# Identity matmuls in a layer's tail and head, an earlier gather, and one wq row ahead of the first scores

## The chip, the cores and the metric

The kernel runs on one core of a Trainium2 chip. The metric is the device time of the program in microseconds (us), taken over several runs. One core has no second core to compare with, so a run counts as fast when it lies within 1.5% of the fastest of its kernel. Executions of one kernel in one call lie up to 4.2 us apart (busy16_only below: 1984.76 to 1988.94).

## The reference, cut to what matters

Four attention blocks for one token: caches A, B, A, B. Each normalises x, makes q from wq, attends to 32 heads of 8192 keys of 192 numbers, and projects by wo.

```python
x = x + _A_ref(_layernorm(x), A_k_cache, A_v_cache, A_wq, A_wo)   # layer 0
x = x + _B_ref(_layernorm(x), B_k_cache, B_v_cache, B_wq, B_wo)   # layer 1
x = x + _A_ref(_layernorm(x), ...)                                # layer 2
x = x + _B_ref(_layernorm(x), ...)                                # layer 3
```

With one token nothing of K and V is used twice within a layer: the program reads 848 MB from HBM.

## The kernel before

Heads go in 16 pairs. For each pair, VectorE (DVE) multiplies K by q in place; TensorE (PE) adds up the products by matmuls with the identity; softmax; PE multiplies by V; DVE picks and PE gathers ("e"); wo is applied in pieces. Loads go through one queue in a fixed order, each as soon as its slot is free. The order of steps at a layer's start and end is a list (cuts marked, comments added):

```python
elif l == 2:
    plan += [("wq", l, g) for g in range(3)]
    steps.append(("wq", l, 0))            # two wq rows ahead of the first scores
...
steps.append(("m", l, p, 0))              # DVE products and PE sums, first half of the keys
if l == 2 and p == 0:
    steps.append(("wq", l, 1))
...
steps.append(("m", l, p, 1))
if l == 2 and p == 0:
    steps.append(("wq", l, 2))
...
plan.insert(-2, ("wo", l, 2))
steps.append(("e", l, p - 1))             # gather of pair 14
steps += [("v", l, p, 0), ("wc", l, 2)] if NB[l] else [("wc", l, 2), ("v", l, p, 0)]
steps += [("wo", l, 2), ("v", l, p, 1)]
if NB[l]:                                 # layers 1 and 3
    plan.append(("vq", l))                # last quarter of pair 15's V
    both(("wob", l))                      # second part of the last large wo piece
steps.append(("e", l, p))                 # gather of pair 15
both(("wol", l))                          # last wo piece, into the row that "wc" frees
```

In layer 2 the slots of the K halves and of the wq pieces are what the next loads go into: the first V load waits for the sums of the first half of K, the third wq piece for the first wq piece's rows.

```python
PE.wait(last["S"][u], ev_const)
for c in range(4):
    PE.wait(chunks[c])                    # a piece of DVE's products
    ...                                   # 6 identity matmuls a piece, 24 in all
freed[nt] = ev_S[p, u] = e                # frees the K half
```

Of the kernel before, what the change touches and what calls it, by code (L numbers as in the profile page):

```python
# [68 lines left out]
def build(nc, A_x, A_k, A_v, A_wq, A_wo, B_x, B_k, B_v, B_wq, B_wo, out):  # L69
    _, H, SK, DH = A_k.shape  # L70
    D = A_x.shape[-1]
    P = 128
# [17 lines left out]
    NB = [0, 5, 0, 5]  # L90
# [7 lines left out]
    with ExitStack() as ctx:  # L98
# [9 lines left out]
        ident = sb("ident", [P, P], BF16)  # L108
# [40 lines left out]
        SP_ = [ps("S0"), ps("S1")]  # L149
# [6 lines left out]
        Su = [(use["S0"],), (use["S1"],)]  # L156
# [60 lines left out]
        def both(*ns):  # L217
            plan.extend(ns)
            steps.extend(ns)

        for l in range(NL):
            if l < 2:
                plan.append(("wq", l, 0))
                steps += [("wq", l, g) for g in range(3)]
            elif l == 2:
                plan += [("wq", l, g) for g in range(3)]
                steps.append(("wq", l, 0))
            else:
                both(("wq", l, 0))
            for p in range(NPAIR):  # L230
                if first_load("k", l, p) == (l, p):
                    plan += [("k", l, p, u) for u in range(2)]
                if stays("k", l, p):
                    plan += [("t", l, p, u) for u in range(2)]
                steps.append(("m", l, p, 0))
                if l == 2 and p == 0:
                    steps.append(("wq", l, 1))
                if l == 2 and p == 1:
                    steps.append(("e", l, 0))
                steps.append(("m", l, p, 1))  # L240
                if l == 2 and p == 0:
                    steps.append(("wq", l, 2))
                if p == NPAIR - 1:
                    steps.append(("v", l, p - 1))
                steps.append(("s", l, p))
                if l == 3 and p == 0:
                    both(("wq", l, 1), ("wq", l, 2))
                if p < NPAIR - 2:
                    if first_load("v", l, p) == (l, p):
                        plan += [("v", l, p, u) for u in range(2)]  # L250
                        if l == 2 and p == 1:
                            i = plan.index(("k", l, 1, 0))
                            plan[i - 1:i + 1] = [("k", l, 1, 0), ("v", l, 0, 1)]
                    steps.append(("v", l, p))
                    if l != 2 or p > 0:
                        steps.append(("e", l, p))
                    if p + 1 in (PAIRS_W, 2 * PAIRS_W):
                        b = (p + 1) // PAIRS_W - 1
                        steps.append(("wc", l, b))
                        both(("wo", l, b))  # L260
            for i in (p - 1, p):
                if first_load("v", l, i) == (l, i):
                    plan += [("v", l, i, u) for u in range(2)]
            plan.insert(-2, ("wo", l, 2))
            steps.append(("e", l, p - 1))
            steps += [("v", l, p, 0), ("wc", l, 2)] if NB[l] else [("wc", l, 2), ("v", l, p, 0)]
            steps += [("wo", l, 2), ("v", l, p, 1)]
            if NB[l]:
                plan.append(("vq", l))
                both(("wob", l))  # L270
            steps.append(("e", l, p))
            both(("wol", l))
        at = {n: i for i, n in enumerate(steps)}

# [137 lines left out]
        ev_true = DV.op(lambda v: v.tensor_copy(x_true[:], x_bf[:]), ev_x)  # L412
        ev_z = DV.op(lambda v: v.tensor_copy(z[:], x_bf[:]), ev_x)

        def sums(ev_z):

            DV.wait(ev_z, last["st"])
            DV.op(lambda v: v.tensor_reduce(st[:, 0:1], z[:], AX.X, ALU.add))
            e = DV.op(lambda v: v.scalar_tensor_tensor(out=zz[:], in0=z[:], scalar=1.0, in1=z[:],
                                                       op0=ALU.mult, op1=ALU.mult, accum_out=st[:, 1:2]))  # L420
            e = PE.op(lambda t: t.matmul(TB[:, C_ST:C_ST + 2], lhsT=ones[:, 0:1].broadcast_to([P, P]), rhs=st[:], start=True, stop=True),
                      e, ev_const, last["stt"], bank=TBu)
            last["st"] = e
            e = DV.op(lambda v: v.tensor_scalar(mv[:], TB[:, C_ST:C_ST + 2], 1.0 / D, None, ALU.mult), e, last["rs"], bank=TBu)
            last["stt"] = e
            return e

        def layer(l, ev_z, ev_true):

            ev_mv = sums(ev_z)  # L430
            if l == 0:
                ev_z = DV.op(lambda v: v.tensor_scalar(z[:], z[:], mv[:, 0:1], None, ALU.subtract), ev_mv)
                ev_mv = sums(ev_z)
            ev_xb = DV.op(lambda v: v.tensor_scalar(xb[:], z[:], mv[:, 0:1], None, ALU.subtract),
                          ev_mv, ev_z, last["xb"])
            e = DV.op(lambda v: v.scalar_tensor_tensor(out=nv[:], in0=mv[:, 0:1], scalar=mv[:, 0:1], in1=mv[:, 1:2],
                                                       op0=ALU.mult, op1=ALU.subtract))
            e = DV.op(lambda v: v.tensor_scalar(vs[:], nv[:], -float(DH), float(DH) * EPS, ALU.mult, ALU.add), e, last["rs"])
# [16 lines left out]
            for c in range(DC):  # L455
                for h in range(2):
                    e = PE.op(lambda t, c=c, h=h: t.matmul(
                        QM[64 * h:64 * h + 64, 0:DH], lhsT=xb[:, c:c + 1].broadcast_to([P, 64]),
                        rhs=q_first[:, c, h * DH:(h + 1) * DH], start=(c == 0), stop=(c == DC - 1)),
                        signal=(c == DC - 1 and h == 1), bank=QMu)  # L460
            ev_q = {}
            i0 = l * NPAIR % 2
            ev_q[0] = last["QB"] = AC.op(
                lambda a: a.activation(q_sb[i0][:], QM[:, 0:DH], ACT.Copy, scale=rs[:, 0:1]),
                e, ev_rs, last["q"][i0], bank=QMu)

            def q_rows(g):

                n = ("wq", l, g)
                c0, k = Q_PARTS[g]  # L470
                t3 = wq_rows(l, g)[:, :, ORDER[l]["q1"] * PD if l < 2 else 0:]
                PE.wait(need(("wq", l, 0)) if l < 2 else need(n), ev_xb, last["O"], last["YB"], ev_first.get(l))
                for c in range(k):
                    for b in range(4):
                        w = min(512, QR - b * 512)
                        for r in range(3):
                            fin = c0 + c == DC - 1
                            o, x, y = (OY[32 * r:32 * r + 1, b * 512:b * 512 + w], xb[:, c0 + c:c0 + c + 1],
                                       t3[:, c, r * QR + b * 512:r * QR + b * 512 + w])
                            e = PE.op(lambda t, b=b, c=c, r=r, o=o, x=x, y=y, fin=fin: (  # L480
                                t.matmul(o, lhsT=x, rhs=y, start=c0 + c == 0, stop=fin) if b == 0 else
                                matmul_held(t, o, x, y, c0 + c == 0, fin, 32, 32 * r)),
                                signal=(c == k - 1 and b == 3 and r == 2), bank=OYu)
                freed[n] = e
                if c0 + k == DC:
                    last["xb"] = e
                    last["rows"] = AC.op(
                        lambda a: a.activation(rows[0:65, :], OY[0:65, 0:QR], ACT.Copy, scale=rs[0:65, 0:1]),
                        e, ev_rs, last["qbc"], bank=OYu)
# [176 lines left out]
            for n in [n for n in steps if n[1] == l]:  # L666
                if n[0] == "m":
                    products(*n[2:])
                elif n[0] == "s":
                    softmax(n[2])  # L670
                elif n[0] == "v":
                    values(n[2], n[3:] or (0, 1))
                elif n[0] == "e":
                    gather(n[2])
                elif n[0] == "wq":
                    q_rows(n[2])
                    q_ready = n[2] == 2 or q_ready
                elif n[0] == "wc":
                    columns(NW)
                    last["oTw"] = last["TT"]  # L680
                elif n[0] == "wo":
                    k = NW - NB[l] if n[2] == 2 else NW
                    last["oT"] = project(n, slot[place[n]][:, 0:k * D], oT[:, 0:k], last["oTw"])
                elif n[0] == "wob":
                    last["oT"] = freed[("wo", l, 2)] = project(
                        n, slot[place[("wo", l, 2)]][:, (NW - NB[l]) * D:NW * D], oT[:, NW - NB[l]:NW], last["oTw"])
                else:
                    last["TT"] = last["TTn"]
                    last["oTl"] = ev_y = project(n, rows[:], oTl, last["TTn"])
                if q_ready and (n[0] == "wq" and l >= 2 or n[0] == "m" and n[3] == 1):  # L690
                    following = n[2] + 1 if n[0] == "m" else 1
                    if following < NPAIR and following not in ev_q:
                        q_spread(following)
                ahead()
# [64 lines left out]
```

## Time and profile before

| | kernel before |
|---|---|
| median of the first 3 runs | 1984.95 us |
| read from HBM | 848 MB at 428 GB/s |
| busy share of PE, DVE | 64%, 61% |
| seam of layers 1 and 2: second wo piece landed, third wq piece landed, first V load issued and landed | 1012.14, 1030.59, 1029.60, 1039.25 us |
| end: last V quarter landed, last DVE instruction ended | 1975.77, 1981.19 us |

A load runs on 16 DMA engines: in this trace 16 packets of the load queue were in flight for 1827.7 of 1982.3 us, and the 183 loads have 2928 semaphore updates, 16 each. "Landed" means the last of the 16. That each update stands for one engine is my reading; no record names an engine. The **hole** is (V load landed) - (third wq piece landed) - 7.30 us, where 7.30 is the spacing of two loads of that size in steady flow: the time that was lost on the slowest DMA engine between the two loads. The prediction works it out for the kernel before, 1.36 us. The **tail** is (last DVE instruction ended) - (layer 3's last V quarter landed), before 81.19 - 75.77 = 5.42 us.

This is the timeline of the kernel before (columns: start, us, engine, line, operation, out<-in, shapes, count, and in brackets the idle time before it and what ended it):

```profile
996.95 3.14 DVE L639 SCALAR_TENSOR_TENSOR acc<-OY,small,acc 128x192 f32<-128x192 f32 x7
...
1000.14 0.81 PE L650 MATMUL TB<-acc,small 128*1 128x192 f32 x4 [4.15 <-DVE acc L639]
...
1002.89 2.73 PE L620 MATMUL OY<-pool,p_sb 128*4 128x384 bf16 x32 [0.66 <-DMA pool<-in_B_v_cache_dram]
```

PE is idle for 4.15 us while DVE picks. At 1001.02 the clock falls to half, and the 32 value matmuls take 2.73 us.

### The profile page before, as it was taken

The page shows a single profiled execution, that of the slowest core. Times are in us where ns is not written, and L with a number is a line of the kernel's source. Part 1 is how long each engine was busy: PE and PEld are TensorE (multiplying, and loading weights), DVE is VectorE, ACT ScalarE, POOL GpSimd, SP SyncE. Part 2 cuts the span into 40 slices and gives each one's busy share as a digit, 9 for nine tenths or more (in the row PEclk, how much of TensorE's full clock was granted, in tenths as well). Part 3 has the DMA queues.
Part 4 walks back from the last instruction along what each step waited for, and adds up shares of the span by engine and source line. Part 5 has one row for each costly group of instructions (what it writes and reads, how often), then busy time and mean ns, then how long its engine had stood idle before and what let it go on. Part 6 is the DMA issues. An engine that isn't in the chain of part 4 may idle for free.

```text
span 1984.0 us, 13908 instructions
## 1 busy us (share of the span) xinstructions
PE 1273.4 (64%) x8310; PEld 150.1 (8%) x3266; DVE 1200.7 (61%) x1371; ACT 139.5 (7%) x461; POOL 4.5 (0%) x22
## 2 busy tenths in 40 slices
PE   3567567566466666665775665675676766656657
PEld 0001001000200100100020010010002001001001
DVE  3566467467166656556745565665664775665665
ACT  0000000000000000000010000000000000000000
POOL 0000000000000000000000000000000000000000
PEclk9787777777587787777876777878886887777777
DMA  9999999999999999999999999999999999999998
GB/s 412 438 430 431 431 437 429 431 430 431 433 435 431 432 429 436 430 431 432 427 388 433 430 430 430 432 430 430 431 431 427 435 432 434 430 432 432 432 431 353
DMA packets 26926, 849.25 MB, mean 428 GB/s; under 512 B 3184, under 2 KB 3184, under 8 KB 3952
## 3 DMA queue, kind: packets, MB, share of 16 engines
q1 hardware_dynamic: 26720, 848.38, 99.5%
q8 instruction: 45, 0.74, 0.2%
q14 instruction: 17, 0.14, 0.0%
q10 hardware_dynamic: 144, 0.00, 0.0%
HBM read 848.36 MB, written 0.00 MB: 428 GB/s over the span
## 4 chain that ended last, share of the span: by engine, by line
DMA 68%; DVE 15%; PE 15%; ACT 1%; issue 0%; SPq 0%
DMA pool<-in_B_k_cache_dram 27%; DMA pool<-in_A_v_cache_dram 20%; DMA pool<-in_A_k_cache_dram 14%; DVE pool L543 13%; PE S L58 6%; PE OY L58 5%; DMA pool<-in_B_v_cache_dram 4%; PE OY L620 3%; DMA pool<-in_B_wo_dram 2%; ACT p_sb L580 1%; DVE acc L639 1%; DMA pool<-in_A_wq_dram 1%; DVE s_sb L565 1%; PE OY L513 0%; PE S L556 0%
## 5 line engine op out<-in xcount | busy, mean ns | idle before, releaser
L543 DVE TENSOR_TENSOR pool<-pool,q_sb 128x3072 bf16<-128x3072 bf16 x512 | 861.2, 1753 | 241.5 <-DMA pool<-in_B_k_cache_dram 144.0
L58 PE MATMUL S<-pool,ident 128*128 128x512 bf16 x2944 | 789.1, 425 | 20.3 <-DVE pool L543 19.0
L650 PE MATMUL TB<-acc,small 128*1 128x192 f32 x240 | 82.1, 493 | 219.1 <-DVE acc L639 219.1
L556 PE MATMUL S<-pool,ident 128*128 128x512 bf16 x128 | 62.9, 491 | 213.6 <-DVE pool L543 213.6
L58 PE MATMUL OY<-pool,p_sb 128*16 128x512 bf16 x1920 | 197.0, 485 | 0.0
L638 DVE TENSOR_SCALAR acc<-OY,small 128x192 f32<-128x192 f32 x64 | 26.7, 418 | 274.2 <-PE OY L58 246.2
L620 PE MATMUL OY<-pool,p_sb 128*16 128x512 bf16 (+1 forms) x1216 | 147.5, 497 | 62.7 <-DMA pool<-in_A_v_cache_dram 56.4
L639 DVE SCALAR_TENSOR_TENSOR acc<-OY,small,acc 128x192 f32<-128x192 f32 x424 | 177.1, 418 | 14.9
L565 DVE TENSOR_REDUCE s_sb<-S 128x64 f32<-128x512 f32 x128 | 88.1, 688 | 69.4 <-PE S L58 69.4
L502 ACT ACTIVATE q_sb<-QM 128x192 bf16<-128x192 f32 x60 | 19.9, 331 | 954.8 <-PE QM L496 954.8
L661 ACT ACTIVATE rows<-TB,small 1x192 bf16<-1x192 f32 x120 | 43.2, 406 | 585.1 <-PE TB L650 585.1
L634 DVE RECIPROCAL small<-TB 1x2 f32<-1x2 f32 x64 | 11.2, 175 | 96.7 <-PE TB L595 75.2
L580 ACT ACTIVATE p_sb<-s_sb,small 64x128 bf16<-64x128 f32 x128 | 55.7, 435 | 161.9 <-DVE small L574 161.1
L556 PEld LDWEIGHTS S<-pool,ident 128*128 128x128 bf16 x128 | 13.0, 101 | 686.2 <-DVE pool L543 636.4
L595 PE MATMUL TB<-small,ones 128*1 128x2 f32 x120 | 11.4, 165 | 74.1 <-ACT p_sb L580 74.1
L620 PEld LDWEIGHTS OY<-pool,p_sb 128*16 128x16 bf16 (+1 forms) x1216 | 39.3, 107 | 203.6 <-issue 133.5
L570 PE MATMUL QM<-ident,m_bf 128*64 128x64 bf16 x128 | 14.1, 217 | 54.4 <-DVE m_bf L567 53.8
L650 PEld LDWEIGHTS TB<-acc,small 128*1 128x1 f32 x240 | 19.7, 101 | 311.4 <-DVE acc L639 283.9
L513 PE MATMUL OY<-oT,pool 128*128 128x1 bf16 x900 | 38.2, 178 | 3.5 <-ACT oT L528 2.8
L513 PEld LDWEIGHTS OY<-oT,pool 128*128 128x128 bf16 x900 | 37.1, 131 | 7.0 <-ACT oT L528 3.6
L574 DVE TENSOR_REDUCE small<-QM 128x1 f32<-128x64 f32 x64 | 14.4, 225 | 36.1 <-PE QM L570 36.1
L496 PEld LDWEIGHTS QM<-rows,one_b 1*64 1x64 bf16 x120 | 6.2, 100 | 350.7 <-issue 344.8
(59 smaller groups left out, 186.1 us busy)
## 6 DMA issues: line engine op xcount, KB each, us to landing
pool<-in_B_k_cache_dram SPq DMA_DIRECT2D x28, 6144.0 KB, 38.1
pool<-in_B_v_cache_dram SPq DMA_DIRECT2D x28, 6144.0 KB, 34.2
pool<-in_A_v_cache_dram SPq DMA_DIRECT2D x27, 6144.0 KB, 27.6
pool<-in_A_k_cache_dram SPq DMA_DIRECT2D x34, 3072.0 KB, 20.4
pool<-in_A_k_cache_dram SPq DMA_DIRECT2D x14, 6144.0 KB, 36.8
pool<-in_A_v_cache_dram SPq DMA_DIRECT2D x10, 3072.0 KB, 14.3
pool<-in_B_k_cache_dram SPq DMA_DIRECT2D x8, 3072.0 KB, 22.7
pool<-in_A_wo_dram SPq DMA_DIRECT2D x6, 2400.0 KB, 21.4
```

Of the source, the lines that this page charges most:

```text
L58: return t.add_instruction(mybir.InstMatmult(name=t.bass.get_next_instruction_name(), engine=mybir.EngineType.PE, ins=[t.lower_ap(rhs), t. ...
L502: lambda a: a.activation(q_sb[i][:], QM[:, 0:DH], ACT.Copy), e, last["q"][i], bank=QMu)
L513: e = PE.op(lambda t, i=i, c=c, f=y_first[0], fin=n[0] == "wol" and i == k - 1: t.matmul(YB[:, c:c + 1], lhsT=t3[:, i, c:D:DC], rhs=o[:, i ...
L543: e = DV.op(lambda v, d0=d0: v.tensor_tensor(k3[:, :, d0:d0 + QD], kin[:, :, d0:d0 + QD], q_sb[qi][:, d0:d0 + QD].unsqueeze(1).broadcast_t ...
L556: t.matmul(S[:, :], lhsT=ident[:], rhs=k3[:, :, d0:d0 + R], start=True, stop=fin) if d0 == 0 else
L565: lambda v, u=u: v.tensor_reduce(s[:, u * JU:(u + 1) * JU], SP_[u][:].rearrange("p (j r) -> p j r", r=R), AX.X, ALU.add), ev_S[p, u], last ...
L580: ev_p[p] = AC.op(lambda a, h=h, r=r: a.activation(p_sb[par][r, :, h], s[r, :], ACT.Exp, bias=negm[par][r, 0:1], accum_out=l_col[par][r, h ...
L620: t.matmul(o, lhsT=x, rhs=y, start=f, stop=fin) if c == 0 else
L638: v.tensor_scalar(acc[:], O[:, 0:DH], pick[:, 0:1], None, ALU.mult) if i == 0 else
L639: v.scalar_tensor_tensor(out=acc[:], in0=O[:, i * DH:(i + 1) * DH], scalar=pick[:, i:i + 1], in1=acc[:], op0=ALU.mult, op1=ALU.add)), e if ...
L650: e = PE.op(lambda t, h=h: t.matmul(TB[96:97, C_O + h * DH:C_O + (h + 1) * DH], lhsT=half[:, h:h + 1], rhs=acc[:], start=True, stop=True), ...
L661: last["TO"] = last["row_written"] = AC.op(lambda a, h=h: a.activation(orow[:, o0 + h * DH:o0 + (h + 1) * DH], TB[96:97, C_O + h * DH:C_O ...
```

## The change

Its intent: keep the TensorE clock up through the tails of layers 1 and 3 and raise it early in layer 2, and get the first scores of layer 2 done sooner, because a V load waits for them. The core of the diff (cuts marked, comments added):

```diff
                 if l == 2 and p == 0:
-                    steps.append(("wq", l, 1))
+                    steps += [("wqr", l, 0), ("wq", l, 1)]
...
-            steps.append(("e", l, p - 1))
+            steps += [("busy", l, 16), ("e", l, p - 1)] if NB[l] else [("e", l, p - 1)]
...
             if NB[l]:
                 plan.append(("vq", l))
+                steps.append(("e", l, p))
                 both(("wob", l))
-            steps.append(("e", l, p))
+            else:
+                steps.append(("e", l, p))
             both(("wol", l))
...
+        def busy(n):                      # n matmuls identity x identity into a score bank, result unused
+            PE.wait(ev_const, last["S"][0])
+            ...
@@ layer 2's normalisation
+            if l == 2:
+                busy(2)                   # after the sums
...
+            if l == 2:
+                busy(6)                   # after the first q
...
-            def q_rows(g):
+            def q_rows(g, r0=0, r1=None): # only rows r0 to r1 of a wq piece
...
-                freed[n] = e
+                freed.setdefault(n, e)    # row one frees its part of the slot
...
                     last["oTl"] = ev_y = project(n, rows[:], oTl, last["TTn"])
+                    if l == 1:
+                        busy(2)           # after the last projection of layer 1
```

More of the change, by code (lines that the diff above doesn't have):

```diff
@@ L413, in build @@
         ev_z = DV.op(lambda v: v.tensor_copy(z[:], x_bf[:]), ev_x)
+        def busy(n):
+            PE.wait(ev_const, last["S"][0])
+            for i in range(n):
+                PE.op(lambda t, i=i: (
+                    t.matmul(SP_[0][:, :], lhsT=ident[:], rhs=ident[:].unsqueeze(1).broadcast_to([P, 4, P]), start=True, stop=True)
+                    if i == 0 else
+                    matmul_held(t, SP_[0][:, :], ident[:], ident[:].unsqueeze(1).broadcast_to([P, 4, P]), True, True)),
+                    signal=False, bank=Su[0])
         def sums(ev_z):
@@ L472, in q_rows @@
                 PE.wait(need(("wq", l, 0)) if l < 2 else need(n), ev_xb, last["O"], last["YB"], ev_first.get(l))
-                for c in range(k):
+                r1 = k if r1 is None else r1
+                for c in range(r0, r1):
                     for b in range(4):
@@ L482, in q_rows @@
                                 matmul_held(t, o, x, y, c0 + c == 0, fin, 32, 32 * r)),
-                                signal=(c == k - 1 and b == 3 and r == 2), bank=OYu)
-                freed[n] = e
+                                signal=(c == r1 - 1 and b == 3 and r == 2), bank=OYu)
+                freed.setdefault(n, e)
                 if c0 + k == DC:
@@ L674, in layer @@
                     gather(n[2])
+                elif n[0] == "busy":
+                    busy(n[2])
+                elif n[0] == "wqr":
+                    q_rows(n[2], 1)
                 elif n[0] == "wq":
-                    q_rows(n[2])
+                    q_rows(n[2], 0, 1 if l == 2 and n[2] == 0 else None)
                     q_ready = n[2] == 2 or q_ready
```

## The prediction

> **What bounds the kernel now.** I read the page first, then the chain of waits in order of time, then the DMA share in small windows, then the timeline of the few places where that share falls.
>
> ```profile
> PE 1273.4 (64%) x8310; PEld 150.1 (8%) x3266; DVE 1200.7 (61%) x1371; ACT 139.5 (7%) x461; POOL 4.5 (0%) x22
> ...
> DMA  9999999999999999999999999999999999999998
> ...
> HBM read 848.36 MB, written 0.00 MB: 428 GB/s over the span
> ...
> DMA 68%; DVE 15%; PE 15%; ACT 1%; issue 0%; SPq 0%
> ```
>
> No compute engine is above 64%, while the DMA row is 9 in 39 of 40 slices and DMA is 68% of the chain. The 848 MB take the span. A change that moves no byte can gain only where the queues run dry. Looking in half-microsecond windows, I find three places: the launch, the seam between layer 1 and layer 2 (1005 to 1031 us), and the end (from 1972 us). The seams before layer 1 and before layer 3 show no hole.
>
> The windows around the middle seam and the end (columns: busy of PE, weight loads, DVE, ACT, POOL, then granted clock, DMA share, GB/s):
>
> ```profile
> 1005.00:1012.00 7.00, 6.45 (x105) 3.85 (x97) 0.39 (x2) 0.19 (x1) 0.00 (x0) 0.50 0.88 343
> 1012.00:1020.00 8.00, 4.49 (x64) 3.88 (x64) 3.28 (x13) 0.69 (x2) 0.55 (x1) 0.50 1.00 421
> ...
> 1024.00:1028.50 4.50, 4.50 (x20) 0.00 (x0) 4.50 (x3) 0.00 (x0) 0.00 (x0) 0.90 0.94 361
> 1028.50:1031.00 2.50, 2.50 (x29) 0.18 (x6) 2.50 (x3) 0.00 (x0) 0.00 (x0) 1.00 0.61 169
> ```
>
> The DMA share is 0.88, 0.94 and 0.61, and the granted TensorE clock is 0.50 through the whole tail of layer 1. Idle share times length: 0.12 x 7 + 0.06 x 4.5 + 0.39 x 2.5 = 2.1 us averaged over the 16 DMA engines. The timeline at the deepest hole:
>
> ```profile
> 1018.57 13.44 DVE L543 TENSOR_TENSOR pool<-pool,q_sb 128x3072 bf16<-128x3072 bf16 x8 [1.11 <-ACT q_sb L464]
> 1020.28 0.09 PEld L481 LDWEIGHTS OY<-pool,xb 128*1 128x1 bf16 x3 [2.56 <-DMA pool<-in_A_wq_dram]
> ...
> 1023.58 0.61 PE L556 MATMUL S<-pool,ident 128*128 128x512 bf16 x1
> 1023.68 0.34 SPq L376 DMA_DIRECT2D pool<-in_A_wq_dram  x1
> 1023.98 5.59 PE L58 MATMUL S<-pool,ident 128*128 128x512 bf16 x23
> ...
> 1029.60 0.34 SPq L371 DMA_DIRECT2D pool<-in_A_v_cache_dram  x1
> ```
>
> DVE multiplies K by q in eight pieces of 1.68 us from 1018.57, so the first half (four pieces) is ready at 1025.3. PE cannot start adding it up until 1023.58, because two wq rows at the half clock stand before it (12 matmuls of 512 columns each, 3.3 us together). It finishes at 1029.5; only then is the slot free and the next V load issued, at 1029.60, when the queues are already drying up. That load is on the path.
>
> **Which engine matters.** A transfer's landing is 16 semaphore updates, and the trace has their times. For the last wo piece of layer 1 they run from 1005.70 to 1012.14: the slowest DMA engine is 6.45 us behind the fastest. Of the 2.1 us above, most is idle time of engines that were ahead anyway. The slowest had its last wq piece landed at 1030.59, and the V load behind it landed at 1039.25. A full-speed load of that size takes 7.30 us (a steady spacing of landings in layer 2: 1045.99 to 1053.29), so its hole is 1039.25 - 7.30 - 1030.59 = **1.36 us**. That is the largest gain I see at the seam if the same engine stays the slowest.
>
> [...]
> - [...] granted clock is 0.5 or 1.0, in pieces of 3.41 us or multiples (1001.02 to 1024.91 is 23.89, seven windows at half).
> [...]
> - [...] The trace shows 45 packets of 16384 bytes of about 1.07 us, and smaller ones of 8192; the spread of landings jumps by about 1 us at the latter (at 425.6, 620.7, 800.0 and 981.2 us). So I take the lag to belong to particular engines in both halves, an inference.
>
> **The change, part by part.**
>
> 1. *Sixteen identity matmuls before the picking of pair 14*, in layers 1 and 3. DVE picks pair 14 from 996.49 to about 1000.1 (one instruction of 0.42 us, then seven in 3.14), and PE is free from 996.0 until 1000.14. At full clock a 512-column matmul takes about 0.22 us (23 in 5.13 us from 1031.45), so 16 take 3.5 us: they fit. They hold the clock up in the window that ended at 1001.02, so it falls one window later, near 1004.4. Then the first half of pair 15's values (32 matmuls from 1002.89, 2.73 us at half clock) may run in half the time. What follows waits for DMA anyway: the last quarter of V lands at 1010.20 and in layer 3 at 1975.77. The second half starts there, cold again, because in this trace no stretch of projection matmuls (75 of them filling 0.99 of a window at 1499) ever raised the clock. So on the path: 0. The wol and wq loads come about 1.3 us sooner, but only for engines that are ahead: 0.
>
> 2. *Gather of pair 15 before the second wo piece*. Before, at the end:
>
> ```profile
> 1977.59 0.42 DVE L638 TENSOR_SCALAR acc<-OY,small 128x192 f32<-128x192 f32 x1 [4.66 <-PE OY L620]
> 1977.74 1.08 PEld L513 LDWEIGHTS OY<-oT,pool 128*128 128x128 bf16 x25 [0.92 <-DMA pool<-in_B_wo_dram]
> ...
> 1978.83 0.96 PEld L646 LDWEIGHTS TB<-small,acc 128*64 128x64 f32 x12
> ...
> 1980.23 0.68 PEld L513 LDWEIGHTS OY<-oTl,rows 128*128 128x128 bf16 x15 [0.44 <-ACT oTl L656]
> ```
>
> The 25 projections (1.08 us) lie beside the DVE's two picks (to 1978.46) and delay the 12 gather matmuls by only 0.37. After: gather 1978.51 to 1979.55, ACT's 0.27 hidden, 25 + 15 projections at 43 ns = 1.72 plus the last one's latency 0.08, to 1981.38; before they ended at 1980.99. **+0.4 us** at the end, on the path. At the seam the same sum gives 1013.75 + 1.8 = 1015.6 against 1015.43: +0.15, and the second wq load, which waits for that wo slot, moves from 1013.3 to about 1014.9; engines ahead are done with the first wq at 1016.96, so it arrives in time.
>
> 3. *busy(2), busy(2), busy(6) around layer 2's normalisation*. At half clock a matmul is 0.43 us, so each pair is 0.86. After wol PE was free for 0.52 us, and between the sums and q for 0.52: if cold, each pair delays the chain by about 0.34. Then q starts at 1018.0 instead of 1017.06 (0.15 + 0.34 + 0.34), DVE at 1019.5. Six more (2.6 us cold) end about 1021.5; the first wq lands at 1020.24, so 1.2 us late. In return the window 1018.1 to 1021.5 is now full and the clock should rise near 1021.5 instead of 1024.91.
>
> 4. *Only one wq row before the first scores*. One row warm is 0.9 to 1.0 us: scores start at 1022.5 to 1023. PE then catches up with DVE (24 x 0.22 = 5.2), so the first half ends 1.47 us after the fourth DVE piece: 1019.5 + 6.75 + 1.5 = **1027.8**, against 1029.5. The V load issues there; from issue to first bytes was 1.3 us (1029.60 to 1030.9), so data come at 1029.1, before the slowest engine dries at 1030.59. Its hole closes nearly whole: **-1.2 us** (1.36 less a margin). The third wq part overwrites only row one's half of the slot, so it may issue at 1022.5 instead of 1023.68; hidden. The other rows move behind the scores (three rows, 2.8 us, 1027.8 to 1030.6, against 1031.2 before), so the second half is not delayed.
>
> Sum: -1.2 (seam) + 0.4 (end) = -0.8; 1984.95 - 0.8 = 1984.1 us.
>
> **Rivals.**
> - *All DMA engines' holes count, not only the slowest's*: if the lag moves among engines, closing the 2.1 us at the seam gains all of it. For: the idle share; against: the jumps sit at regular fetches. With a warm tail too: about 1982.5.
> - *A new wait at the seam*: the extra matmuls stay cold and hold back q, so DVE becomes the bound (its 6.75 us start later) and the V load still issues after 1029. For: seven windows at half clock; against: one wq row (1.7 us cold) is taken out before it. Gain 0.3, loss 0.4 at the end: about 1985.
> - *The clock stays up through both tails*: pair 15's second half then takes 0.7 us less after its V has landed, and the reordering pays (-0.3 at the end instead of +0.4). Against: projections did not raise it. About 1983.3.
> - *Hidden anyway*: equal within the repeat spread, 1984.85 to 1985.31.
>
> **Range and chances.** Most rivals lie between 1982.5 and 1985.3, so the range is 1982.7 to 1985.3. Two per cent is 40 us, while all idle of the queues at seam and end is under 10: faster 0.01, same 0.98, slower 0.01.
>
> **What would show it.** In the changed trace: the V load after the first scores issues near 1027.8 and the window before 1031 has no 0.61; the clock falls about one window later after pair 14 but is 0.5 again at the second half of pair 15; pair 15's gather stands before the 25 projections and the end after the last landing is 0.4 us longer; layer 3's last V quarter lands about 1.2 us earlier than 1975.77. I am wrong if these landings move by 2 us or more (then the idle of all engines counted), or by none (then the fourth DVE piece came too late), or if the tails are warm.

Arguments about the clock, the fetches and the projections rest on these measurements of the kernel before:

- *Windows.* In the 202 clock records, the first apart, the clock changes only at multiples of 3.413 us, to within 4 ns; such a stretch is what the text calls a window. There are 568 whole ones. At half clock, PE was busy for 80% or more in 116, and 98 of these were followed by full clock; it was busy for under 70% in 124, and none of these was. At full clock, all 203 with PE busy for 50% or more were followed by full clock, and all 91 with under 40% by half. None of the 16 at half clock with over 1 us of projections was followed by full clock. What decides is not shown beyond these counts.
- *Matmuls.* Identity matmuls of 512 columns start 0.427 us apart at half clock (1023.98 to 1024.41) and 0.216 at full (1031.45 to 1031.67).
- *Fetches.* The page lists 45 packets (of 16384 bytes, median 1.069 us) and 17 (of 8192 bytes) under queues of the kind "instruction". At the four times named, the spread of a load's updates goes from 2.81 to 3.76 us, from 3.78 to 4.76, from 4.77 to 5.74 and from 5.83 to 6.78.

## The result, and the profile after

The median of 6 runs is 1984.93 us (1984.38 to 1985.44); the kernel before has 1985.51 over 6 runs (1984.85 to 1986.53). The ratio is 0.9997, with a 95% interval of 0.9984 to 1.001. A ratio here is the mean time of one kernel's fast runs over that of the other's of the same rounds, so it is not quite the ratio of the medians. The interval is some 5 us wide: the times say "same" and no more.

The page of the changed kernel, the same rows:

```profile
PE 1276.7 (64%) x8352; PEld 149.3 (8%) x3271; DVE 1200.5 (61%) x1371; ACT 139.5 (7%) x461; POOL 4.4 (0%) x22
...
DMA  9999999999999999999999999999999999999998
...
HBM read 848.36 MB, written 0.00 MB: 428 GB/s over the span
...
DMA 67%; DVE 16%; PE 16%; ACT 1%; issue 0%; SPq 0%
```

PE has 42 instructions more (16 + 16 + 10) and 3.3 us more busy time. The bytes and the bound are as they were. The windows at the seam (busy of PE, weight loads, DVE, ACT, POOL, then granted clock, DMA share, GB/s):

```profile
1005.00:1012.00 7.00, 5.55 (x98) 3.61 (x97) 1.00 (x3) 0.19 (x1) 0.00 (x0) 0.74 0.88 332
1012.00:1020.00 8.00, 7.96 (x80) 4.01 (x70) 3.11 (x12) 0.69 (x2) 0.55 (x1) 0.57 0.98 392
...
1024.00:1028.50 4.50, 4.29 (x43) 0.27 (x9) 4.50 (x4) 0.00 (x0) 0.00 (x0) 1.00 1.08 449
1028.50:1031.00 2.50, 2.50 (x19) 0.10 (x1) 2.50 (x2) 0.00 (x0) 0.00 (x0) 1.00 0.91 372
```

The last window's DMA share went from 0.61 to 0.91 (a share a little over 1, such as 1.08, comes from records that overlap: 17 packets of the load queue at once for 83.5 us of this trace). The first window is still at 0.88: that hole was not closed. The timeline there; lines of the kernel have moved, L543 to L560, L556 to L573, L481 to L498, L371 to L373:

```profile
1018.12 13.44 DVE L560 TENSOR_TENSOR pool<-pool,q_sb 128x3072 bf16<-128x3072 bf16 x8 [1.40 <-ACT q_sb L480]
1019.73 0.09 PEld L498 LDWEIGHTS OY<-pool,xb 128*1 128x1 bf16 x3 [2.07 <-DMA pool<-in_A_wq_dram]
...
1020.64 0.39 PE L573 MATMUL S<-pool,ident 128*128 128x512 bf16 x1
1020.87 3.86 PE L58 MATMUL S<-pool,ident 128*128 128x512 bf16 x17
1024.94 1.46 PE L58 MATMUL S<-pool,ident 128*128 128x512 bf16 x6 [0.21 <-DVE pool L560]
...
1026.43 0.34 SPq L373 DMA_DIRECT2D pool<-in_A_v_cache_dram  x1
```

The first wq row takes 0.9 us instead of 3.3 for two. PE then catches up with DVE and even waits for it (0.21), and the V load issues at 1026.43 instead of 1029.60. The clock rose at 1018.95; before it rose at 1024.91.

The 16 matmuls, and the end (L620 is now L637, L638 L655, L646 L663, L513 L530), again from the timeline of the changed kernel:

```profile
995.78 3.40 PE L58 MATMUL S<-ident 128*128 128x512 bf16 x15
...
999.77 0.81 PE L667 MATMUL TB<-acc,small 128*1 128x192 f32 x4 [0.59 <-DVE acc L656]
...
1967.87 1.47 PE L637 MATMUL OY<-pool,p_sb 128*4 128x384 bf16 x32
...
1975.14 1.45 PE L637 MATMUL OY<-pool,p_sb 128*4 128x384 bf16 x16 [1.62 <-DMA pool<-in_B_v_cache_dram]
1976.64 0.42 DVE L655 TENSOR_SCALAR acc<-OY,small 128x192 f32<-128x192 f32 x1 [5.82 <-PE OY L637]
...
1977.57 1.04 PE L663 MATMUL TB<-small,acc 128*64 128x1 f32 x12 [0.98 <-DVE acc L656]
```

The 16 fit beside DVE's picking: PE waits 0.59 us instead of 4.15 and starts the gather no later. In layer 3 the first 32 value matmuls take 1.47 us instead of 2.73, and the last 16 now wait 1.62 us for their V quarter. The gather stands before the 25 projections.

Yet the landings did not move as predicted. From the second wo piece at the seam to layer 3's last V quarter it was 1975.77 - 1012.14 = 963.63 us before and is 1975.10 - 1011.42 = 963.68 after. The hole at the seam, computed as above, is still 38.51 - 30.06 - 7.30 = 1.15 us, although the V load was issued 3.2 us sooner. And the tail is 5.40 us where I had expected 5.8. In this one profile the seam gained nothing on the slowest DMA engine and the end lost nothing: both of my terms failed, in opposite directions. That the time still lies in the range is luck, and says little: the range (1982.7 to 1985.3) also holds the kernel before, at 1984.95 in its first three runs. Was the missing gain the rule or chance?

### The profile page after: what moved, and what is told of

Read it like the earlier page. It is cut to its first block, busy times and chain, and to the rows that moved or that the text cites. A ratio compares the mean times of both kernels' runs of the same rounds, so it can differ in the third digit from the quotient of the medians.

```text
span 1983.6 us, 13955 instructions
## 1 busy us (share of the span) xinstructions
PE 1276.7 (64%) x8352; PEld 149.3 (8%) x3271; DVE 1200.5 (61%) x1371; ACT 139.5 (7%) x461; POOL 4.4 (0%) x22
## 4 chain that ended last, share of the span: by engine, by line
DMA 67%; DVE 16%; PE 16%; ACT 1%; issue 0%; SPq 0%
DMA pool<-in_B_k_cache_dram 27%; DMA pool<-in_A_v_cache_dram 20%; DMA pool<-in_A_k_cache_dram 14%; DVE pool L560 14%; PE S L58 7%; DMA pool<-in_B_v_cache_dram 6%; PE OY L58 5%; PE OY L637 3%; DVE acc L656 1%; ACT p_sb L597 1%; DVE s_sb L582 1%; PE S L573 0%; PE OY L530 0%; DVE m_bf L584 0%; PE QM L587 0%
## 5 line engine op out<-in xcount | busy, mean ns | idle before, releaser
L560 DVE TENSOR_TENSOR pool<-pool,q_sb 128x3072 bf16<-128x3072 bf16 x512 | 861.1, 1754 | 241.0 <-DMA pool<-in_B_k_cache_dram 142.8
L573 PE MATMUL S<-pool,ident 128*128 128x512 bf16 x128 | 62.2, 486 | 213.9 <-DVE pool L560 213.9
L655 DVE TENSOR_SCALAR acc<-OY,small 128x192 f32<-128x192 f32 x64 | 26.8, 418 | 278.0 <-PE OY L58 247.8
L637 PE MATMUL OY<-pool,p_sb 128*16 128x512 bf16 (+1 forms) x1216 | 147.0, 492 | 64.2 <-DMA pool<-in_A_v_cache_dram 57.8
L573 PEld LDWEIGHTS S<-pool,ident 128*128 128x128 bf16 x128 | 12.9, 101 | 684.7 <-DVE pool L560 659.9
L637 PEld LDWEIGHTS OY<-pool,p_sb 128*16 128x16 bf16 (+1 forms) x1216 | 39.1, 106 | 206.2 <-issue 133.7
L530 PE MATMUL OY<-oT,pool 128*128 128x1 bf16 x900 | 38.2, 178 | 2.8 <-ACT oT L545 2.8
L530 PEld LDWEIGHTS OY<-oT,pool 128*128 128x128 bf16 x900 | 37.1, 131 | 4.9 <-ACT oT L545 3.6
L513 PEld LDWEIGHTS QM<-rows,one_b 1*64 1x64 bf16 x120 | 6.2, 100 | 349.4 <-issue 343.5
```

The source lines that it names most:

```text
L530: e = PE.op(lambda t, i=i, c=c, f=y_first[0], fin=n[0] == "wol" and i == k - 1: t.matmul(YB[:, c:c + 1], lhsT=t3[:, i, c:D:DC], rhs=o[:, i ...
L560: e = DV.op(lambda v, d0=d0: v.tensor_tensor(k3[:, :, d0:d0 + QD], kin[:, :, d0:d0 + QD], q_sb[qi][:, d0:d0 + QD].unsqueeze(1).broadcast_t ...
L573: t.matmul(S[:, :], lhsT=ident[:], rhs=k3[:, :, d0:d0 + R], start=True, stop=fin) if d0 == 0 else
L637: t.matmul(o, lhsT=x, rhs=y, start=f, stop=fin) if c == 0 else
L655: v.tensor_scalar(acc[:], O[:, 0:DH], pick[:, 0:1], None, ALU.mult) if i == 0 else
```

## The experiments

The theories, as the expectations name them. **S**: only the hole of the slowest DMA engine counts, and the change closes it. **F**: that hole stays, and only engines that were ahead gain. **A**: idle time of all 16 engines counts. For the tail: does the new order cost 0.4 us, or nothing? For each kernel the time is the median of its runs, with that of the kernel before.

### Both kernels again, and the V load delayed

No edit for the first two. For the other two:

```diff
-                steps.append(("wq", l, 0))
+                steps += [("wq", l, 0), ("busy", l, 12)]     # or 30; layer 2 only
```

> The kernel before, unchanged, for a second profile and the repeat spread. Every theory: ratio 1.000 within 0.001. The question is the landings: in the first profile the last landing of the second wo piece of layer 1 and the last landing of layer 3's last V quarter are 963.63 us apart (changed kernel: 963.68, so no gain across the seam on the slowest DMA engine). If that spacing varies by over 0.5 us between profiles of the same kernel, one profile of each can't tell the seam's gain.

> The changed kernel again. Theory S (the slowest DMA engine's hole of 1.36 us at the seam closes): 1.2 us shorter spacing from wo landing to layer 3's last V quarter than the kernel before in the same call, time about 1 us less. Theory F (the hole closes only for engines that were ahead; the slowest keeps a stall of about 1.2 us at its first V packet): same spacing within 0.3, time within 0.5 us. Theory A (all engines' idle counts): 2 us or more.

> Changed kernel with 12 more identity matmuls between the first wq row and the first scores, so that the V load behind the scores issues about 2 to 2.6 us later, near 1029, where the kernel before issued it. Theory S: gives back 1.0 to 1.3 us. Theory F: within 0.5 us of the changed kernel. Theory A: gives back 2 us.

> Changed kernel with 30 such matmuls: the V load issues about 6.5 us later than in the changed kernel, near 1033, after every DMA engine has run dry. All theories: a hole on every engine of some 3 us beyond that of the kernel before. Time 3 to 5 us above the changed kernel (S, F: 4.0 to 4.5; A: 5 to 6). If it is under 1 us the queues are not what bounds the seam.

Measured (kernel before: 1986.23 us, 1984.41 to 1987.41, 9 runs):

| kernel | time, us | V load issued | hole, us | tail, us |
|---|---|---|---|---|
| before, again | 1985.50 | 1028.58 | 1.05 | 5.96 |
| changed, again | 1984.66 | 1026.38 | 0.01 | 5.41 |
| 12 more matmuls | 1986.33 | 1028.52 | 1.29 | 5.41 |
| 30 more matmuls | 1989.93 | 1032.65 | 4.88 | 5.41 |

The two profiles of the kernel before differ by 0.6 us in the long spacing (963.63 and 963.02), so my first comparison could not carry a verdict. Between the second profiles it came 0.45 us shorter in the changed kernel, which lies between S (1.2) and F (under 0.3). The hole tells more: it is 1.05 to 1.36 where the V load issues between 1028.5 and 1029.6, and 0.01 in the second profile of the changed kernel. Delaying the V load by 2.1 us brings the hole back (1.29) and with it 1.7 us of time; delaying it by 6.3 us makes it 4.88 and costs 5.3 us. So F falls as the rule, and the seam bounds the time.

What is the hole made of? The trace has the start and the duration of each DMA packet, but not its engine. A V packet of 24576 bytes takes 0.912 us (median), and the load has 128: 8 for each of 16 engines, 8 x 0.912 = 7.30 us, the measured spacing. In the kernel before, the last wq packet ended at 1030.29, the 16 engines' first V packets started between 1030.58 and 1031.54, and 14 of these took 1.29 to 1.79 us. So the slowest engine was idle for 0.3 us or more, and slow first packets came on top. In its second profile the first V packets started from 1029.55 to 1030.09, before the last update of the wq piece at 1030.10. Hardly any engine was idle, 15 of the 16 first packets took 1.4 to 1.95 us, and the hole was still 1.05. In all seven profiles with the V load issued at 1028.5 or later, 12 to 15 of the first 16 V packets took over 1.25 us; with the V load issued by 1027.2 it was 4 to 8. So a late V load costs more than idle time: nearly all engines then start on it together, and slowly. Why a first packet is then slow is not shown.

Why then 1.15 in the first profile of the changed kernel? A V packet that started at 1029.73, when the slowest engines took up the V load, took 2.086 us, 1.17 more than the median, and the last of the V load's 16 updates came 1.13 us after the one before it. So the late engine seems to have met such a slow packet, in one of the seven profiles with an early V load.

Both delays cost more than S expected and less than A: hold12 1.7 us (S 1.0 to 1.3, A 2), hold30 5.3 us (S 4.0 to 4.5, A 5 to 6). In the long spacing they cost 1.9 and 6.4 us. So S against A was still open.

### The parts alone, and the order

no_reorder takes the new order out of the changed kernel; reorder_only puts it alone into the kernel before; split_only puts only the wq split into the kernel before:

```diff
@@ no_reorder, from the changed kernel
-                steps.append(("e", l, p))
                 both(("wob", l))
-            else:
-                steps.append(("e", l, p))
+            steps.append(("e", l, p))
@@ reorder_only: the reverse, in the kernel before
@@ split_only, in the kernel before
-                    steps.append(("wq", l, 1))
+                    steps += [("wqr", l, 0), ("wq", l, 1)]
-                    q_rows(n[2])
+                    q_rows(n[2], 0, 1 if l == 2 and n[2] == 0 else None)
@@ hold_wol, in the changed kernel
-            steps += [("v", l, p, 0), ("wc", l, 2)] if NB[l] else ...
+            steps += [("v", l, p, 0)] + [("busy", l, 8)] * (l == 1) + [("wc", l, 2)] if NB[l] else ...
```

> Changed kernel with pair 15's gather back behind the second wo piece in layers 1 and 3. From the last landing of layer 3's last V quarter to the end of the last vector instruction it took 5.41 us in four profiles of the changed kernel's tail, and 5.42 and 5.96 in two of the kernel before. If the prediction's +0.4 for the new order holds, this tail is 5.0. If the tail is bound by the landing of the second wo piece (1.9 us after the V quarter) in the old order, it is 5.4 and the order is worth nothing. Time within 0.6 us of the changed kernel.

> Kernel before with the new order alone (no identity matmuls, no split of the wq rows). PE's values of pair 15 end 1.8 to 2.6 us after the V quarter's landing (clock at half), against 1.5 in the changed kernel, so tail 5.7 to 6.5 us: 0.3 us or more longer than the kernel before. Seam unchanged: V load issued at 1028.5 to 1029.8, hole on the slowest DMA engine over 1 us. Time 0 to 1 us above the kernel before.

> Kernel before with the split of the first wq rows alone. One row at half clock ends about 1022.0; the V load behind the first scores issues at 1027 to 1028. Theory S (only the slowest DMA engine's hole counts): the V load lands 26.0 to 26.4 us after the second wo piece, against 27.1 and 26.8 before and 26.0 in the changed kernel, so the split alone carries most of the seam's gain, and time is about 1 us below the kernel before. If the identity matmuls are needed for it, the V load issues after 1028.5 and nothing is gained.

> Changed kernel with 8 identity matmuls in layer 1 only, ahead of the transposes whose end frees the row that the last wo piece is loaded into: the DMA engines that are ahead stand idle 2 to 3 us longer near 1006, the slowest one does not. Theory S: the V load lands 26.0 (to 26.4) us after the second wo piece, time within 0.5 us of the changed kernel. Theory A (idle time of all engines counts): 1 to 1.5 us more in time and from wo piece to layer 3's last V quarter.

Measured (kernel before: 1985.77 us, 1985.45 to 1988.66, 7 runs):

| kernel | time, us | V load issued | hole, us | tail, us |
|---|---|---|---|---|
| no_reorder | 1984.68 | 1026.56 | 0.01 | 5.39 |
| reorder_only | 1987.02 | 1029.24 | 0.69 | 5.81 |
| split_only | 1986.08 | 1029.00 | 1.80 | 6.09 |
| hold_wol | 1984.45 | 1026.42 | -0.01 | 5.40 |

**The order is worth nothing in the changed kernel**: 5.39 us of tail without it, 5.40 to 5.41 with it. The predicted cost of 0.4 is refuted. The timeline of no_reorder has what binds the old order: the 25 projections wait for the second wo piece.

```profile
1974.47 1.45 PE L635 MATMUL OY<-pool,p_sb 128*4 128x384 bf16 x16 [0.63 <-DMA pool<-in_B_v_cache_dram]
...
1976.38 1.16 PE L528 MATMUL OY<-oT,pool 128*128 128x1 bf16 x25 [0.45 <-DMA pool<-in_B_wo_dram]
```

In the kernel before (reorder_only) the tail of 5.81 us lies between that kernel's two (5.42 and 5.96), so nothing is shown there. This run missed two expectations: its hole is 0.69 and not over 1, and its time 1.25 us above the kernel before and not up to 1.

**The split alone doesn't do it.** Its expectation was missed: the V load issued at 1029.00, not at 1027 to 1028. The timeline of split_only shows why:

```profile
1022.12 0.61 PE L567 MATMUL S<-pool,ident 128*128 128x512 bf16 x1
...
1022.51 6.45 PE L58 MATMUL S<-pool,ident 128*128 128x512 bf16 x23
...
1029.00 0.34 SPq L371 DMA_DIRECT2D pool<-in_A_v_cache_dram  x1
```

The sums start 1.5 us sooner than before, but at half clock: the 23 take 6.45 us, since with one row fewer ahead of them the clock still rose only at 1025.2. The gain in the start is nearly all lost in the run. Its hole of 1.80 is not idle time alone either: the first V packets started at 1029.96, before the wq piece's last update at 1031.33.

**hold_wol is inconclusive.** It did issue the last wo piece 2.0 us later than the changed kernel's second profile (4.76 against 6.78 us before the landing of the second wo piece), but the engines that are ahead only stood idle earlier instead of later: the mean idle time over the 16 engines from 8 us before that landing to 28 after it (36 us less a sixteenth of all packets' time) is 0.59 against 0.61 us. It can't tell S from A.

### The matmuls alone

busy16_only and seambusy_only are the kernel before with only the 16 ahead of pair 14's picking, and with only the ten around layer 2's normalisation. no16 is the changed kernel without the 16:

```diff
@@ no16
-            steps += [("busy", l, 16), ("e", l, p - 1)] if NB[l] else [("e", l, p - 1)]
+            steps.append(("e", l, p - 1))
```

> Kernel before with the 16 identity matmuls ahead of pair 14's picking alone (layers 1 and 3). Tail from the landing of layer 3's last V quarter: 5.4 us (the values of pair 15 are on time, 1.5 us after the landing), against 5.42 to 5.96 before. Seam: the clock is at half again by layer 2's normalisation, so the two wq rows and the first scores are slow and the V load issues at 1028.5 to 1029.8; hole on the slowest DMA engine over 1 us. Time 0 to 0.5 us below the kernel before.

> Kernel before with the ten identity matmuls around layer 2's normalisation alone. They should raise the clock one window sooner (near 1021 instead of 1023 to 1025), so that both wq rows and the first scores run at full clock: V load issued at 1027.3 to 1028.3, hole on the slowest DMA engine 0.3 us or less. If they cost what the prediction feared (q later by 0.7 us), DVE's fourth piece binds and the V load issues after 1028.3. Tail as in the kernel before, 5.4 to 6.0.

> Changed kernel without the 16 identity matmuls. Tail 5.7 to 6.2 us as with the new order alone (5.81 there). Seam: with the split and the ten identity matmuls the V load issues at 1026.5 to 1028; the slowest DMA engine has no hole (wq landing to V landing 7.3 to 7.5 us unless a packet stalls). Time 0.3 to 0.7 us above the changed kernel.

Measured (kernel before: 1986.02 us, 1984.74 to 1986.82, 7 runs):

| kernel | time, us | V load issued | hole, us | tail, us |
|---|---|---|---|---|
| busy16_only | 1985.55 | 1029.50 | 1.63 | 5.46 |
| seambusy_only | 1984.97 | 1027.16 | 0.06 | 6.02 |
| no16 | 1985.50 | 1026.84 | 0.00 | 6.06 |

This takes the change apart. **The ten matmuls at the normalisation close the hole**, even with both wq rows ahead of the scores:

```profile
1020.06 0.38 PE L496 MATMUL OY<-pool,xb 128*1 128x512 bf16 x3
...
1022.00 5.13 PE L58 MATMUL S<-pool,ident 128*128 128x512 bf16 x23
...
1027.16 0.34 SPq L371 DMA_DIRECT2D pool<-in_A_v_cache_dram  x1
```

That is seambusy_only: 5.13 us for the 23 sums, at full clock since 1019.7. The split brings the V load forward by another 0.3 to 0.8 us, which no hole was left to use in these profiles. **The 16 matmuls shorten the tail**: 5.39 to 5.46 us in all eight profiles that have them (late_wol below included), 5.42, 5.96, 5.81, 6.09, 6.02 and 6.06 in the six that lack them. The second profile of the kernel before shows what they remove:

```profile
1968.44 2.73 PE L620 MATMUL OY<-pool,p_sb 128*4 128x384 bf16 x32
...
1974.54 2.73 PE L620 MATMUL OY<-pool,p_sb 128*4 128x384 bf16 x32
```

The last V quarter landed at 1974.69, but PE, late by its slow first half, had only begun the quarter before it. There is no wait for a DMA in the second line. In the changed kernel that line is cut in two by a wait of 1.62 us for the landing: PE is on time.

### All engines or the slowest

The last run delays the first of layer 2's loads by another route, so that the engines ahead lose time and the slowest does not:

```diff
-                before[n] = [("wc", n[1], 2)]
+                before[n] = [("late", 1) if n[1] == 1 else ("wc", n[1], 2)]
...
+                            if l == 1 and p == NPAIR - 1 and r == rounds * 3 // 4 - 1 and g == G - 1:
+                                freed[("late", 1)] = e
```

> Changed kernel in which layer 1's last wo piece, and with it the first wq rows behind it in the queue, is issued only when three quarters of pair 15's values are done (2 to 4 us later than in the changed kernel, still before the slowest DMA engine is through with the second wo piece). The engines that are ahead stand idle some 1 to 1.5 us more in the mean of the 16 (0.6 to 1.0 us in four profiles with an early V load), the slowest none. Theory S: no hole on the slowest (wq landing to V landing 7.3 us), V load 25.8 to 26.2 us after the second wo piece, time still below the kernel before and within 0.5 us of the changed kernel (1.0 to 1.5 below the kernel before). Theory A (idle time of all engines counts): the seam's gain is given back, time within 0.5 us of the kernel before, and layer 3's last V quarter lands 1 us or more later behind the wo piece than in the changed kernel.

Its windows, the first and the last of those shown before:

```profile
1005.00:1012.00 7.00, 4.34 (x83) 2.73 (x83) 1.00 (x3) 0.00 (x0) 0.00 (x0) 0.74 0.79 311
...
1028.50:1031.00 2.50, 2.50 (x19) 0.10 (x1) 2.50 (x2) 0.00 (x0) 0.00 (x0) 1.00 0.94 371
```

The DMA share of the first window fell to 0.79, and the mean idle time in the stretch defined above rose from 0.61 to 1.34 us. The hole is 37.49 - 30.19 - 7.30 = 0.00, the V load landed 26.02 us after the second wo piece (26.00 in the changed kernel's second profile), layer 3's last V quarter 962.38 us after it (962.57 there), and the time is 1984.39 us against 1985.79 of the kernel before. The idle time rose by 0.7 us, less than the 1 to 1.5 expected, and that cost nothing that these numbers show. For an idle time of this size S holds and A does not. The extra cost of hold30, whose hole was 4.88 us and whose time rose by 5.3, is not explained by S.

All profiles together say what the seam is worth. From the second wo piece to layer 3's last V quarter it took 962.38 to 963.17 us (mean 962.72) in the six with the V load issued by 1027.2 and no hole, and 963.02 to 964.03 (mean 963.61) in the five that delay nothing and issue it from 1028.5 to 1029.6. That is 0.9 us, where the mean hole of those five is 1.3.

## Why the prediction was right or wrong

The time lay in the range: 1984.93 against 1984.1, and 0.58 below the kernel before's median where 0.8 was predicted. As said above, that is luck in the first profile. My own sign of being wrong, landings that don't move, came true there (963.63 and 963.68). By its own steps:

- **Bound and place: right.** The bytes are the bound, and only the seam and the end had room. The V load behind the first scores is the load on the path: delayed, it costs 1.7 and 5.3 us, a little more than the hole grows by (1.3 and 4.9).
- **Only the slowest DMA engine's hole counts: right for what the change does**, by late_wol, where 0.7 us more of idle time cost nothing. hold30 cost more than its hole. The inference that the lag stays with the same engines is not shown; no run names an engine.
- **-1.2 at the seam: right as a rule for the hole, missed in the first profile, and for another reason in part.** The hole went from 1.36 and 1.05 to 0.01 (and to 0.06 or less in five more profiles with the V load issued by 1027.2), but 1.15 was left where one packet was slow; in the spacing the gain is 0.9. I had the data reach the slowest engine too late. From issue to first packet I read 1.3 us, but the first packet started at 1030.58, after 0.97; and in the second profile of the kernel before it came in time and the hole was there. What I left out is that the first packets are slow when nearly all engines start on the load together: 14 of 16 took 1.29 to 1.79 us there, against a median of 0.912.
- **V load at 1027.8: too late by 1.4 us.** The rule was right: fourth DVE piece plus 1.47 us, 1018.12 + 6.75 + 1.47 = 1026.34. Mis-sized was "the extra matmuls delay q by 0.34 and 0.34, the order by 0.15". From the landing of layer 1's last V quarter to DVE's start it was 1018.57 - 1010.20 = 8.37 us before and 1018.12 - 1009.50 = 8.62 after: 0.25, not 0.83. That is 0.6 of the 1.4; another 0.7 is that the V quarter itself landed 0.70 us earlier in that execution, and 0.1 is rounding.
- **Credit in the wrong part.** I had given the gain to the split and treated the ten matmuls as a cost that buys a clock. Alone, the ten close the hole and the split does not.
- **The 16 matmuls worth 0 at the end: wrong.** The step that failed was "what follows waits for DMA anyway". In the first profile the value matmuls of the second half ran through without a pause (only their weight loads waited 0.28 us for the V quarter), and in the second there is no wait at all. The matmuls take 0 to 0.6 us off the tail. I had also expected one more stretch of 3.41 us at full clock; in layer 3 the clock fell at 1974.7 and 1973.3, against 1967.0 and 1965.4 before, 7.7 and 7.9 us later, so the tail was warm in part. In layer 1 of the first profile it fell at 1001.9, hardly later than before, and rose again at 1005.3.
- **+0.4 for the order: wrong.** I took the values' end from the kernel before, 1.77 us after the V quarter's landing. On time they end 1.50 us after it, and in the old order the projections then wait for the second wo piece, which lands 1.9 us after that quarter. Both orders come to 5.4 us.

The sum of the hole and tail terms, as the runs have them, is -1.0 to -1.4 and 0 to -0.6. The medians differ by 0.6 and 1.6 us. The times agree with that but could not have shown it.

Left open: in the changed kernel the last 16 value matmuls still run at half clock (1.45 us, against 0.82 for the 16 before them) on the path at the very end. Matmuls in the 1.6 us wait before them might gain some half a us, an estimate from those two times (1.45 - 0.82 = 0.63, if the clock rose); no run tried it.

## What to carry to other kernels

In a kernel that is bound by its loads, ask of a matmul that does no work which load it brings forward: here ten of them at the head of a layer were worth about 0.9 us of a load's landing because a freed slot, and so a load, waited behind sums at half clock (the 23 sums took 5.59 us before, 5.13 with the ten). Measure a hole on the slowest DMA engine, from landing to landing, not by the mean share of 16 engines, and look at the packets before you call it idle time. And when the effect is smaller than the spread of the times, choose a stretch in the profile that the change must shorten, and take more than one profile of each kernel before believing it.

## What else the traces show

- Busy time alone doesn't tell whether the clock rises. In the kernel before, a stretch at half clock (1625.66 to 1629.07) in which PE was busy for 2.72 us, all of it with identity matmuls of 512 columns, was followed by full clock. Another (1973.82 to 1977.23), in which PE was busy throughout, 2.43 us with value matmuls of 384 columns and the rest with projections of one column, was followed by half clock. Why is not shown.
- The spread of landings adds up and goes again: in the kernel before the 16 updates of one load spread over 1.25 us at the launch (22.16), over 6.45 us in the load that landed at 1012.14, and over 0.56 us after the hole, in the V load that landed at 1039.25.
- An instruction fetch is seen on the load queue: in the kernel before, a packet of 49152 bytes that started at 425.9 us, just after a fetch packet of 8192 bytes at 425.58, took 2.478 us, against a median of 1.819. After each of the 17 fetch packets of that size in the span, a packet that started 0.3 to 0.4 us later took 0.38 to 0.66 us more than the median of its size.
- The first packets after a late V load are slow: of the first 16 V packets of 24576 bytes, 12 to 15 took over 1.25 us (median of the kernel before's load: 0.912) in the seven profiles that issue the V load at 1028.5 or later (14 in the kernel before), and 4 to 8 in the seven that issue it by 1027.2 (4 in the changed kernel).
